# Query products of a linear-attention and two-layer kernel: four 64x64 blocks of TensorE in place of one 128x128 block-diagonal product

## The chip, the cores and the metric

The kernel runs on one core of one Trainium2 chip. The metric is the device time of one execution in microseconds (us). Before the change it is 289.2 us, the median of three runs (289.18 to 289.35).

## The reference

Inputs are q, k and v, each [8 batches, 8 heads, 576 positions, 64 channels] in float32, and the weights w_in [512, 2048] and w_out [2048, 512]. For each batch and head:

```python
q_s = softmax(q, axis=channels)
k_s = softmax(k, axis=positions)
kv  = k_s^T @ v          # 64 x 64 for each head
x   = q_s @ kv           # 576 x 64 for each head
```

The eight heads' x are laid side by side, which gives 4608 tokens of 512 channels, and then

```python
h   = x @ w_in
out = maximum(0.01 * h, h) @ w_out      # 4608 x 512, float32
```

## The kernel before

All of w_in, w_out and x (transposed: channels on partitions, tokens along the free dimension, tile `xT`) stay in on-chip memory as bf16. The two dense layers are worked through in nine tiles of 512 tokens, t = 0 to 8. In a tile, `layer1` (L459) makes sixteen blocks `ph` of 128 hidden units, each with four matmuls over the four 128-row blocks of channels; `leaky` (L469) takes each from PSUM through ScalarE into `gj`; then `layer2` (L481) makes four blocks `pout` of 128 tokens, sixteen matmuls each. The first tile is different: it covers batch 0's 576 positions, its first 256 columns are begun with half of the channel blocks (`begin`, L659) before the rest is there.

Beside this dense work the attention of the next batches is prepared. For a batch b:

- `kv` (L291; for batch 0 `kv_pair`, L368) multiplies exp(k) with v. The contraction over 64 positions of a row uses half of TensorE's rows, so two matmuls with 64 rows and 128 columns, one on each half of the rows, stand one behind the other, 36 for a batch. A product of 128x128 holds two heads on its diagonal 64x64 blocks; what is off the diagonal is not wanted.
- `kd_make` (L309; for batch 0 `kd_rec` and `kd_one`, L382 and L386) divides the diagonal blocks by the sums of exp(k) and writes them into `kd2`, four 128x128 block-diagonal tiles for a batch. The zeros off the diagonal were written once (L124). `kd_one` multiplies a whole 128x128 tile with a mask `block` (L106).
- `q_turn` (L436) turns the softmax of q so that channels lie on partitions, with a DMA transpose on SyncE's queue (for batch 0 `q_transpose` on TensorE and `q_keep`, L393 and L409).
- `attend_x` (L444; for batch 0 `attend`, L417) multiplies: one 128x128 matmul for each pair of heads and each of two parts of the positions (`XR`: 320 and 256 columns), eight for a batch, each into a PSUM tile of its own, which ScalarE (for batch 1 also VectorE) copies into `xT`.

The order is written out by hand. Each engine works through its instructions in the program's order. The `at(t, u, ...)` table hangs pieces of attention work behind unit u of tile t: units 0 to 15 are the blocks of layer 1, units 16 to 31 groups of four layer-2 matmuls. `attend_x` stands in four units, two matmuls in each, in layer 2 of some tile (L597 for batch 1: two units of four; L637 for batch 2; L619 for the others).

PSUM has two pools: `psB` with six buffers of one bank (`ph`, `pkv`, `po`, the transposes) and `psO` with two (`pout`).

At the start GpSimd's queue loads w_in with a cast from float32 to bf16, in two halves (L520, L547), each as four transfers of 64 partitions (`load_w_in`, L130). The halves are put behind parts of k by small copies into `gate`. SyncE's queue loads q, k and v of batch 0, then a small transfer `held` (L514, called at L575) that waits for the first w_in transfer of the second half, and behind it k, q and v of batch 1. GpSimd waits for batch 1's k (L579) before it issues w_out in six transfers (L141).

In this kernel channel block c of `w_in_sb` holds heads in the order that the block-diagonal tiles give (`XB`, and the rearrangement at L127), so w_in's rows are permuted when they are loaded.

Of the kernel before, what the change touches and what calls it, by code (L numbers as in the profile page):

```python
# [8 lines left out]
FP32 = mybir.dt.float32  # L9
BF16 = mybir.dt.bfloat16  # L10
AF = mybir.ActivationFunctionType
ALU = mybir.AluOpType
# [7 lines left out]
L = 64  # L20
R = 9
# [4 lines left out]
def kernel(  # L26
# [78 lines left out]
    make_identity(nc, identf)  # L105
    block = const_pool.tile([P, P], FP32)  # L106
    nc.gpsimd.memset(block, 0.0)
    for p0 in range(0, P, D):
        nc.gpsimd.memset(block[p0 : p0 + D, p0 : p0 + D], 1.0)
    warm = const_pool.tile([P, 1], BF16)  # L110
# [5 lines left out]
    xT = xT_pool.tile([P, NB, T], BF16)  # L116
    XB = (0, 2, 1, 3)


    vb2 = [const_pool.tile([P, R, 2, 130], BF16, name=f"vb{i}") for i in range(2)]  # L120
    kd2 = [const_pool.tile([P, NB, P], BF16, name=f"kd{i}") for i in range(2)]
    for i in range(2):
        nc.gpsimd.memset(vb2[i][:, :, :, 128:129], 1.0)
        nc.gpsimd.memset(kd2[i], 0.0)  # L124


    w_in_r = moe_w_in.rearrange("(gg hp hh d) f -> gg hp d hh f", gg=2, hp=2, hh=2)  # L127
    w_in_t = w_in_sb.rearrange("p (hh gg) f -> p gg hh f", gg=2)

    def load_w_in(j0, j1):  # L130
        fs = slice(j0 * P, j1 * P)
        for gg in range(2):
            for hp in range(2):
                nc.gpsimd.dma_start(  # L134
                    out=w_in_t[hp * D : (hp + 1) * D, gg, :, fs], in_=w_in_r[gg, hp, :, :, fs]
                )

# [171 lines left out]
    def kd_make(b):  # L309
        for hh in range(2):  # L310
            pkv = st[b]["pkv"][hh]
            krec = small_pool.tile([P, 2, 1], FP32, name="krec")
            nc.vector.reciprocal(out=krec, in_=pkv[:, :, 128:129])
            for hp in range(2):
                p0 = hp * D
                nc.vector.tensor_tensor(
                    out=kd2[b % 2][p0 : p0 + D, 2 * hh : 2 * hh + 2, p0 : p0 + D],
                    in0=pkv[p0 : p0 + D, :, p0 : p0 + D],
                    in1=krec[p0 : p0 + D].to_broadcast([D, 2, D]),
                    op=ALU.mult,  # L320
                )
# [63 lines left out]

    def kd_one(eng, b, gg, hh):  # L386
        pkv, krec = st[b]["pkv", gg][hh], st[b]["krec", gg, hh]
        o = kd2[b % 2][:, 2 * hh + gg]
        eng.scalar_tensor_tensor(
            out=o, in0=pkv[:, 0:P], scalar=krec, in1=block, op0=ALU.mult, op1=ALU.mult  # L390
        )

# [23 lines left out]

    def attend(b, gs, c0, n, eng, pool=psB_pool, tag=BANK_TAG):  # L417

        ps = pool.tile([P, len(gs), n], FP32, name="po", tag=tag)
        for i, g in enumerate(gs):  # L420
            nc.tensor.matmul(  # L421
                ps[:, i],
                lhsT=kd2[b % 2][:, g],
                rhs=st[b]["qT", g % 2][:, g // 2].rearrange("c r l -> c (r l)")[:, c0 : c0 + n],
                start=True,
                stop=True,
            )
        x0 = XB[gs[0]]
        o = xT[:, x0 : x0 + len(gs), b * S + c0 : b * S + c0 + n]
        if eng is nc.scalar:  # L430
            eng.copy(out=o, in_=ps)
        else:
            eng.tensor_copy(out=o, in_=ps)


    def q_turn(b, rs=ALLR):  # L436
# [6 lines left out]

    def attend_x(b, g, rs, eng):  # L444
        hh, gg = divmod(g, 2)
        n = (rs.stop - rs.start) * L
        ps = psB_pool.tile([P, n], FP32, name="po", tag=BANK_TAG)
        qX = st[b]["qX"].rearrange("c (r g) (h l) -> c g h r l", g=2, h=2)
        nc.tensor.matmul(  # L449
            ps.rearrange("p (r l) -> p r l", l=L), lhsT=kd2[b % 2][:, g], rhs=qX[:, gg, hh, rs]  # L450
        )
        c0 = b * S + rs.start * L
        o = xT[:, XB[g], c0 : c0 + n]
        if eng is nc.scalar:
            eng.copy(out=o, in_=ps)  # L455
        else:
            eng.tensor_copy(out=o, in_=ps)

    def layer1(j, ph, c0, n, part=slice(0, 4), first=True, last=True):  # L459
        for i, cb in list(enumerate((0, 2, 1, 3)))[part]:  # L460
            nc.tensor.matmul(  # L461
                ph,
                lhsT=w_in_sb[:, cb, j * P : (j + 1) * P],
                rhs=xT[:, XB[cb], c0 : c0 + n],
                start=(i == 0 and first),
                stop=(i == NB - 1 and last),
            )
# [87 lines left out]
    for hh in range(2):  # L555
        kd_rec(0, 0, hh)
        kd_one(nc.vector, 0, 0, hh)
    q_keep(nc.scalar, 0, 0, 4, (0,))
    attend(0, [0, 2], 0, 256, nc.scalar)
    wake(2)  # L560
# [4 lines left out]
    kd_rec(0, 1, 1)  # L565
    kd_one(nc.vector, 0, 1, 0)
    kd_one(nc.vector, 0, 1, 1)
    q_exp(0, R1)
# [13 lines left out]


    at(0, 9, lambda: attend(0, [0, 2], 256, 256, nc.scalar))
    at(0, 9, lambda: attend(0, [1, 3], 256, 256, nc.vector))
    at(0, 9, lambda: attend(0, [0, 2, 1, 3], 512, 64, nc.scalar, psO_pool, "pout"))
    at(0, 15, lambda: k_begin(1), lambda: q_begin(1), lambda: k_tree(1, H0), lambda: k_tree(1, H1))
# [8 lines left out]
    at(0, 43, lambda: q_turn(1, XR[1]), lambda: load_all(2))  # L596
    for i in range(8):  # L597
        eng = (nc.scalar, nc.vector)[i % 2]
        at(0, (45, 46)[i // 4], lambda i=i, eng=eng: attend_x(1, (0, 2, 1, 3)[i % 4], XR[i // 4], eng))

# [4 lines left out]
    def plan(b, o):  # L605
        t = b - 2
        at(t, o, lambda: k_begin(b), lambda: q_begin(b), lambda: k_tree(b, ALLH))
        at(t, o + 3, lambda: k_allmax(b), lambda: k_sub(nc.gpsimd, b, ALLH))
        at(t, o + 7, lambda: q_max(b, ALLR), lambda: q_sub(nc.gpsimd, b, ALLR))
        at(t, o + 11, lambda: k_exp(b, ALLH))  # L610
        at(t, o + 12, lambda: v_cast(nc.gpsimd, b, 0), lambda: v_cast(nc.gpsimd, b, 1))
        at(t, o + 16, lambda: q_exp(b, ALLR))
        at(t, o + 18, lambda: q_sum(b, ALLR))
        at(t, o + 21, lambda: q_norm(b, ALLR))
        kvu, pu = o + 25, o + (33 if b == 3 else 34)
        at(t, kvu, lambda: kv(b))
        at(t, kvu + 1, lambda: kd_make(b))
        at(t, o + 22, lambda: q_turn(b))
        for i in range(8):  # L619
            at(t, pu + i // 2, lambda i=i: attend_x(b, i // 2, XR[i % 2], nc.scalar))  # L620


    def plan2():
# [12 lines left out]
        at(1, 24, lambda: kd_make(b))  # L636
        for i in range(8):  # L637
            at(1, 28 + i // 2, lambda i=i: attend_x(b, i % 4, XR[i // 4], nc.scalar))

# [25 lines left out]
    for j in range(0, 8, 2):  # L665
        begin(j)
        if j == 2:
            attend(0, [1, 3], 0, 256, nc.scalar)
    q_exp(0, R2)
# [90 lines left out]
```

## Time and profile before

| What | Value |
|---|---|
| median of three runs | 289.2 us |
| span of the profiled execution | 287.8 us |
| outside that span (289.2 less 287.8) | 1.4 us |
| TensorE matmul (PE) busy | 277.4 us, 96%, 1620 instructions |
| VectorE (DVE) busy | 148.9 us, 52% |
| ScalarE (ACT) busy | 148.1 us, 51% |
| GpSimd (POOL) busy | 85.6 us, 30% |
| L449 matmuls `po<-qX,kd` | 56 instructions, 11.1 us busy, mean 286 ns |
| L421 matmuls `po<-qT,kd` (batch 0) | 12 instructions |
| L298 matmuls `pkv<-vb,ke` (64 rows) | 252 instructions |
| granted TensorE clock | 1.00 throughout the span |

Matmuls are pipelined: one that the profile shows with 379 ns for 512 columns starts 216 ns after the one before it. So it is starts that are to be compared, not the durations of single matmuls. A few matmul records are missing from the trace; weight loads (PEld) are complete. The chain of work that ended last follows the releasers back from the last instruction and puts every stretch of the span down to an engine and line.

### The profile page before, as it was taken

The numbers are of one execution on the slowest core, as the hardware profiler recorded it, in microseconds if no ns is written. First come the engines' busy times: TensorE is split into PE (matmuls) and PEld (weight loads), VectorE is DVE, ScalarE is ACT, GpSimd is POOL, SyncE is SP. The second block draws the span as 40 slices with busy tenths as digits, with TensorE's granted clock in tenths as the row PEclk, the third lists the DMA queues.
The fourth block names the chain that finished last, engine by engine and source line by source line (L and its number), as shares of the span: only waits on it lengthen the run. The fifth ranks groups of instructions, "written<-read, shape, count | busy, mean of one in ns | idle before, by whom it ended". The sixth has DMA issues, their size and how long they took to land.

```text
span 287.8 us, 4248 instructions
## 1 busy us (share of the span) xinstructions
PE 277.4 (96%) x1620; PEld 138.6 (48%) x1646; DVE 148.9 (52%) x246; ACT 148.1 (51%) x273; POOL 85.6 (30%) x70
## 2 busy tenths in 40 slices
PE   8689999999999999999999999999999999999995
PEld 3267645555444544454454445454455444444443
DVE  2996975987960993588085727563621100110011
ACT  4976881685269218913764358434843066016400
POOL 4734560026078019406900590049100000000000
PEclk9999999999999999999999999999999999999999
DMA  7999996999959166943496239913141310131033
GB/s 247 321 207 361 271 190 153 394 292 354 173 132 400 36 136 155 397 99 76 91 394 163 67 80 356 219 36 81 30 82 36 75 36 1 39 85 24 0 73 75
DMA packets 38932, 46.35 MB, mean 161 GB/s; under 512 B 18304, under 2 KB 21632, under 8 KB 38912
## 3 DMA queue, kind: packets, MB, share of 16 engines
q1 hardware_dynamic: 35456, 41.75, 49.6%
q0 software_dynamic: 3296, 4.20, 8.4%
q8 instruction: 13, 0.21, 0.3%
q10 hardware_dynamic: 160, 0.13, 0.1%
q14 instruction: 7, 0.06, 0.1%
HBM read 36.70 MB, written 9.44 MB: 160 GB/s over the span
## 4 chain that ended last, share of the span: by engine, by line
PE 90%; DMA 3%; issue 1%; DVE 1%; POOL 1%; ACT 0%; ACTq 0%; POOLq 0%
PE pout L482 43%; PE ph L461 41%; DMA w_in_sb<-in_moe_w_in_dram 3%; PE pkv L298 3%; PE po L449 2%; DVE k_raw L364 1%; POOL w_in_sb L134 0%; ACT gj L470 0%; PE po L421 0%; ACT xT L455 0%; DVE out_sb L476 0%; POOL gate L546 0%; ACTq L470 0%; POOLq L546 0%
## 5 line engine op out<-in xcount | busy, mean ns | idle before, releaser
L482 PE MATMUL pout<-w_out_sb,gj 128*128 128x512 bf16 (+2 forms) x580 | 129.1, 373 | 0.7 <-issue 0.2
L461 PE MATMUL ph<-xT,w_in_sb 128*128 128x512 bf16 (+3 forms) x627 | 126.6, 357 | 2.3 <-DMA w_in_sb<-in_moe_w_in_dram 1.2
L470 ACT ACTIVATE gj<-ph 128x512 bf16<-128x512 f32 (+2 forms) x152 | 83.5, 582 | 55.7 <-PE ph L461 53.9
L461 PEld LDWEIGHTS <-w_in_sb 128*128 128x128 bf16 x640 | 62.1, 98 | 63.5 <-issue 2.4
L482 PEld LDWEIGHTS <-gj 128*128 128x128 bf16 x592 | 57.1, 98 | 62.1
L476 DVE COPY out_sb<-pout 128x512 f32<-128x512 f32 (+1 forms) x34 | 22.7, 674 | 85.2 <-PE pout L482 79.0
L196 POOL TENSOR_TENSOR k_raw<-k_raw,kall 128x2304 f32<-128x2304 f32 x5 | 25.3, 5064 | 76.7 <-DVE kall L188 50.4
L455 ACT CAST xT<-po 128x320 bf16<-128x320 f32 (+1 forms) x52 | 18.2, 402 | 48.6 <-PE po L449 48.6
L276 DVE TENSOR_REDUCE qsum<-qe 128x36 f32<-128x2304 bf16 (+4 forms) x11 | 19.8, 1798 | 32.6 <-ACT qe L267 32.6
L259 POOL TENSOR_TENSOR q_raw<-q_raw,qmax 128x2304 f32<-128x2304 f32 (+3 forms) x10 | 29.7, 2973 | 20.3 <-DVE qmax L228 20.2
L283 DVE TENSOR_TENSOR qe<-qe,qrec 128x2304 bf16<-128x2304 bf16 (+4 forms) x12 | 21.9, 1826 | 0.4
L204 ACT ACTIVATE ke<-k_raw 128x2304 bf16<-128x2304 f32 (+2 forms) x11 | 17.5, 1594 | 8.6 <-POOL k_raw L196 8.5
L228 DVE TENSOR_REDUCE qmax<-q_raw 128x36 f32<-128x2304 f32 (+4 forms) x11 | 19.6, 1790 | 0.1
L267 ACT ACTIVATE qe<-q_raw 128x2304 bf16<-128x2304 f32 (+4 forms) x11 | 16.8, 1526 | 1.1 <-POOL q_raw L259 0.9
L216 POOL CAST vb<-v_raw 128x1152 bf16<-128x1152 f32 x13 | 14.6, 1147 | 0.0
L449 PE MATMUL po<-qX,kd 128*128 128x320 bf16 (+1 forms) x56 | 11.1, 286 | 0.1
L327 PE MATMUL pout<-zero 128*128 128x512 bf16 x27 | 9.1, 475 | 1.3 <-POOL zero L101 1.3
L163 DVE TENSOR_TENSOR t<-k_raw 128x1024 f32<-128x1024 f32 (+1 forms) x10 | 10.1, 1011 | 0.5 <-DMA k_raw<-in_k_dram 0.2
L163 DVE TENSOR_TENSOR t<-t 128x256 f32<-128x256 f32 (+2 forms) x20 | 9.6, 478 | 0.7
L476 ACT COPY out_sb<-pout 128x512 f32<-128x512 f32 (+1 forms) x3 | 1.6, 544 | 14.2 <-PE pout L482 14.2
L298 PEld LDWEIGHTS <-ke 64*128 64x128 bf16 x252 | 7.2, 93 | 3.0 <-ACT gj L470 1.7
L449 PEld LDWEIGHTS <-kd 128*128 128x128 bf16 x56 | 5.5, 98 | 6.2
(61 smaller groups left out, 104.6 us busy)
## 6 DMA issues: line engine op xcount, KB each, us to landing
out_dram<-out_sb SPq DMA_DIRECT2D x70, 128.0 KB, 2.4
q_raw<-in_q_dram SPq DMA_DIRECT2D x7, 1152.0 KB, 8.4
v_raw<-in_v_dram SPq DMA_DIRECT2D x7, 1152.0 KB, 11.6
k_raw<-in_k_dram SPq DMA_DIRECT2D x6, 1152.0 KB, 5.9
k_raw<-in_k_dram SPq DMA_DIRECT2D x4, 576.0 KB, 5.8
w_in_sb<-in_moe_w_in_dram POOLq DMA_DIRECT2D x8, 256.0 KB, 7.1
v_raw<-in_v_dram SPq DMA_DIRECT2D x2, 576.0 KB, 7.6
w_out_sb<-in_moe_w_out_dram POOLq DMA_DIRECT2D x4, 256.0 KB, 9.3
```

Source lines behind the costliest of these rows:

```text
L163: nc.vector.tensor_tensor(out=o, in0=i0, in1=i1, op=ALU.max)
L196: eng.tensor_tensor(out=ks, in0=ks, in1=st[b]["kall"][:, hs].unsqueeze(2).to_broadcast([P, n, R, D]), op=ALU.subtract,)
L228: nc.vector.tensor_reduce(out=m, in_=st[b]["q"][:, :, rs], axis=AX.X, op=ALU.max)
L259: eng.tensor_tensor(out=qs, in0=qs, in1=st[b]["qmax", rs.start].unsqueeze(3).to_broadcast([P, HL, n, D]), op=ALU.subtract,)
L276: nc.vector.reduce_sum(out=qsum, in_=st[b]["qe"][:, rs], axis=AX.X)
L283: nc.vector.tensor_tensor(out=qes, in0=qes, in1=st[b]["qrec", rs.start].unsqueeze(3).to_broadcast([P, n, HL, D]), op=ALU.mult,)
L449: nc.tensor.matmul(ps.rearrange("p (r l) -> p r l", l=L), lhsT=kd2[b % 2][:, g], rhs=qX[:, gg, hh, rs])
L455: eng.copy(out=o, in_=ps)
L461: nc.tensor.matmul(ph, lhsT=w_in_sb[:, cb, j * P : (j + 1) * P], rhs=xT[:, XB[cb], c0 : c0 + n], start=(i == 0 and first), stop=(i == NB - ...
L470: nc.scalar.activation(out=o, in_=ph, func=AF.Prelu, alpha=LEAKY_SLOPE)
L476: copy(out=out_sb, in_=pout)
L482: nc.tensor.matmul(pout, lhsT=g_sb[j // 2][:, j % 2, tsub * P : (tsub + 1) * P], rhs=w_out_sb[:, j, os], start=(j == 0), stop=(j == NF - 1),)
```

## The change

- `kd2` holds only the diagonal 64x64 blocks: tiles of [128, 4, 64] in place of [128, 4, 128]. The mask `block`, its memsets and the zeroing of `kd2` are gone. `kd_one` is two VectorE instructions of 64x64 in place of one of 128x128.
- Each matmul of `attend` and `attend_x` on a 128x128 block-diagonal tile becomes two on 64x64 blocks. `quads` issues four together: two halves of the rows (hp) times two halves of the columns (hh), each with its own 64x64 weights and its own moving data. The two row halves write to different PSUM tiles, the two column halves to different partitions of one tile.
- The order of heads in `xT` becomes the natural one, so w_in's rows are no longer permuted: `load_w_in` issues two transfers of 128 partitions in place of four of 64, four in all in place of eight.
- `attend_x` takes a list of parts. Batches 3 to 7 do all sixteen matmuls in one unit, with six PSUM tiles of `psB`, and the six copies (four of 320 columns, two of 2x256) behind them on ScalarE. Batch 1 and batch 2 do one part in each of two units. Batch 0's late part is two groups of 320 columns in place of pieces of 256 and 64.

```diff
-    kd2 = [const_pool.tile([P, NB, P], BF16, name=f"kd{i}") for i in range(2)]
+    kd2 = [const_pool.tile([P, NB, D], BF16, name=f"kd{i}") for i in range(2)]
...
-    w_in_r = moe_w_in.rearrange("(gg hp hh d) f -> gg hp d hh f", gg=2, hp=2, hh=2)
-    w_in_t = w_in_sb.rearrange("p (hh gg) f -> p gg hh f", gg=2)
+    w_in_r = moe_w_in.rearrange("(c p) f -> p c f", p=P)
...
-        for gg in range(2):
-            for hp in range(2):
-                nc.gpsimd.dma_start(
-                    out=w_in_t[hp * D : (hp + 1) * D, gg, :, fs], in_=w_in_r[gg, hp, :, :, fs]
-                )
+        for cs in (slice(0, 2), slice(2, 4)):
+            nc.gpsimd.dma_start(out=w_in_sb[:, cs, fs], in_=w_in_r[:, cs, fs])
...
+    def quads(b, gg, ps, src, shape=None):
+
+        for hp in range(2):
+            for hh in range(2):
+                o = ps[hp][hh * D : (hh + 1) * D]
+                nc.tensor.matmul(
+                    o if shape is None else shape(o),
+                    lhsT=kd2[b % 2][hp * D : (hp + 1) * D, 2 * hh + gg],
+                    rhs=src(hh)[hp * D : (hp + 1) * D],
+                    start=True,
+                    stop=True,
+                )
+
+    def attend(b, gg, c0, n, engs, pool=psB_pool, tag=BANK_TAG):
+
+        ps = [pool.tile([P, n], FP32, name="po", tag=tag) for _ in range(2)]
+        qT = st[b]["qT", gg]
+        quads(b, gg, ps, lambda hh: qT[:, hh].rearrange("c r l -> c (r l)")[:, c0 : c0 + n])
+        for hp in range(2):
+            move(engs[hp], xT[:, 2 * gg + hp, b * S + c0 : b * S + c0 + n], ps[hp])
...
+    def attend_x(b, parts, engs):
+
         qX = st[b]["qX"].rearrange("c (r g) (h l) -> c g h r l", g=2, h=2)
...
+        made = []
+        for i in parts:
+            rs = XR[i]
+            n = (rs.stop - rs.start) * L
+            cols = slice(b * S + rs.start * L, b * S + rs.stop * L)
+            per = 512 // n
+            for g0 in range(0, 2, per):
+                ps = [psB_pool.tile([P, per, n], FP32, name="po", tag=BANK_TAG) for _ in range(2)]
+                for gg in range(g0, g0 + per):
+                    quads(
...
+                for hp in range(2):
+                    c = 2 * g0 + hp
+                    made.append((xT[:, c : c + 2 * per - 1 : 2, cols], ps[hp]))
+        for i, (o, p) in enumerate(made):
+            move(engs[i % len(engs)], o, p)
...
-    at(0, 9, lambda: attend(0, [0, 2], 256, 256, nc.scalar))
-    at(0, 9, lambda: attend(0, [1, 3], 256, 256, nc.vector))
-    at(0, 9, lambda: attend(0, [0, 2, 1, 3], 512, 64, nc.scalar, psO_pool, "pout"))
+    at(0, 9, lambda: attend(0, 0, 256, 320, (nc.scalar, nc.vector)))
+    at(0, 9, lambda: attend(0, 1, 256, 320, (nc.scalar, nc.vector), psO_pool, "pout"))
...
-    for i in range(8):
-        eng = (nc.scalar, nc.vector)[i % 2]
-        at(0, (45, 46)[i // 4], lambda i=i, eng=eng: attend_x(1, (0, 2, 1, 3)[i % 4], XR[i // 4], eng))
+    for i in range(2):
+        at(0, (45, 46)[i], lambda i=i: attend_x(1, (i,), (nc.scalar, nc.vector)))
...
-        for i in range(8):
-            at(t, pu + i // 2, lambda i=i: attend_x(b, i // 2, XR[i % 2], nc.scalar))
+        at(t, pu + 1, lambda: attend_x(b, (0, 1), (nc.scalar,)))
...
-        for i in range(8):
-            at(1, 28 + i // 2, lambda i=i: attend_x(b, i % 4, XR[i // 4], nc.scalar))
+        for i in range(2):
+            at(1, 28 + 2 * i, lambda i=i: attend_x(b, (i,), (nc.scalar,)))
```

More of the change, by code (lines that the diff above doesn't have):

```diff
@@ L105 @@
     make_identity(nc, identf)
[L106 to L109, printed above, removed]
     warm = const_pool.tile([P, 1], BF16)
@@ L116 @@
     xT = xT_pool.tile([P, NB, T], BF16)
-    XB = (0, 2, 1, 3)
     vb2 = [const_pool.tile([P, R, 2, 130], BF16, name=f"vb{i}") for i in range(2)]
-    kd2 = [const_pool.tile([P, NB, P], BF16, name=f"kd{i}") for i in range(2)]
+    kd2 = [const_pool.tile([P, NB, D], BF16, name=f"kd{i}") for i in range(2)]
     for i in range(2):
         nc.gpsimd.memset(vb2[i][:, :, :, 128:129], 1.0)
-        nc.gpsimd.memset(kd2[i], 0.0)
-    w_in_r = moe_w_in.rearrange("(gg hp hh d) f -> gg hp d hh f", gg=2, hp=2, hh=2)
-    w_in_t = w_in_sb.rearrange("p (hh gg) f -> p gg hh f", gg=2)
+    w_in_r = moe_w_in.rearrange("(c p) f -> p c f", p=P)
     def load_w_in(j0, j1):
         fs = slice(j0 * P, j1 * P)
-        for gg in range(2):
-            for hp in range(2):
-                nc.gpsimd.dma_start(
-                    out=w_in_t[hp * D : (hp + 1) * D, gg, :, fs], in_=w_in_r[gg, hp, :, :, fs]
-                )
+        for cs in (slice(0, 2), slice(2, 4)):
+            nc.gpsimd.dma_start(out=w_in_sb[:, cs, fs], in_=w_in_r[:, cs, fs])
     w_out_r = moe_w_out.rearrange("(fb f) o -> f fb o", f=P)
@@ L316, in kd_make @@
                 nc.vector.tensor_tensor(
-                    out=kd2[b % 2][p0 : p0 + D, 2 * hh : 2 * hh + 2, p0 : p0 + D],
+                    out=kd2[b % 2][p0 : p0 + D, 2 * hh : 2 * hh + 2],
                     in0=pkv[p0 : p0 + D, :, p0 : p0 + D],
@@ L384, in kd_rec, with kd_one @@
         nc.vector.reciprocal(out=krec, in_=st[b]["pkv", gg][hh][:, 128:129])
-    def kd_one(eng, b, gg, hh):
+    def kd_one(b, gg, hh):
         pkv, krec = st[b]["pkv", gg][hh], st[b]["krec", gg, hh]
[L388 to L391, printed above, removed]
+        for hp in range(2):
+            rows = slice(hp * D, (hp + 1) * D)
+            nc.vector.tensor_scalar(
+                out=kd2[b % 2][rows, 2 * hh + gg],
+                in0=pkv[rows, hp * D : (hp + 1) * D],
+                scalar1=krec[rows],
+                scalar2=None,
+                op0=ALU.mult,
+            )
     def q_transpose(b, r0, n):
@@ L415, in q_keep, with move @@
                 eng.tensor_copy(out=o, in_=i)
[L417 to L429, printed above, removed]
+    def move(eng, o, i):
         if eng is nc.scalar:
-            eng.copy(out=o, in_=ps)
+            eng.copy(out=o, in_=i)
         else:
-            eng.tensor_copy(out=o, in_=ps)
+            eng.tensor_copy(out=o, in_=i)
+    def quads(b, gg, ps, src, shape=None):
[8 more added lines that the diff above has]
+                    stop=True,
+                )
+    def attend(b, gg, c0, n, engs, pool=psB_pool, tag=BANK_TAG):
[4 more added lines that the diff above has]
+            move(engs[hp], xT[:, 2 * gg + hp, b * S + c0 : b * S + c0 + n], ps[hp])
     def q_turn(b, rs=ALLR):
@@ L442, in q_turn @@
         )
[L444 to L447, printed above, removed]
+    def attend_x(b, parts, engs):
         qX = st[b]["qX"].rearrange("c (r g) (h l) -> c g h r l", g=2, h=2)
[L449 to L457, printed above, removed]
+        made = []
[8 more added lines that the diff above has]
+                    quads(
+                        b,
+                        gg,
+                        [p[:, gg - g0] for p in ps],
+                        lambda hh: qX[:, gg, hh, rs],
+                        lambda o: o.rearrange("p (r l) -> p r l", l=L),
+                    )
+                for hp in range(2):
+                    c = 2 * g0 + hp
+                    made.append((xT[:, c : c + 2 * per - 1 : 2, cols], ps[hp]))
+        for i, (o, p) in enumerate(made):
+            move(engs[i % len(engs)], o, p)
     def layer1(j, ph, c0, n, part=slice(0, 4), first=True, last=True):
-        for i, cb in list(enumerate((0, 2, 1, 3)))[part]:
+        for i in range(NB)[part]:
             nc.tensor.matmul(
                 ph,
-                lhsT=w_in_sb[:, cb, j * P : (j + 1) * P],
-                rhs=xT[:, XB[cb], c0 : c0 + n],
+                lhsT=w_in_sb[:, i, j * P : (j + 1) * P],
+                rhs=xT[:, i, c0 : c0 + n],
                 start=(i == 0 and first),
@@ L556 @@
         kd_rec(0, 0, hh)
-        kd_one(nc.vector, 0, 0, hh)
+        kd_one(0, 0, hh)
     q_keep(nc.scalar, 0, 0, 4, (0,))
-    attend(0, [0, 2], 0, 256, nc.scalar)
+    attend(0, 0, 0, 256, (nc.scalar, nc.scalar))
     wake(2)
@@ L565 @@
     kd_rec(0, 1, 1)
-    kd_one(nc.vector, 0, 1, 0)
-    kd_one(nc.vector, 0, 1, 1)
+    kd_one(0, 1, 0)
+    kd_one(0, 1, 1)
     q_exp(0, R1)
@@ L667 @@
         if j == 2:
-            attend(0, [1, 3], 0, 256, nc.scalar)
+            attend(0, 1, 0, 256, (nc.scalar, nc.scalar))
     q_exp(0, R2)
```

## The prediction

> **What bounds the kernel now.** I read the chain of work that ended last first, then TensorE's waits, then single stretches of the timeline. The page's chain:
>
> ```profile
> PE 90%; DMA 3%; issue 1%; DVE 1%; POOL 1%; ACT 0%; ACTq 0%; POOLq 0%
> ...
> L449 PE MATMUL po<-qX,kd 128*128 128x320 bf16 (+1 forms) x56 | 11.1, 286 | 0.1
> ```
>
> 90% of the span is TensorE. From the 25 us mark to the end TensorE hardly waits, so there each removed 0.1 us of TensorE is 0.1 us of the span. The L449 row shows 56 products with only 0.1 us of idle time before them: they stand on the path, among dense work. What one visit to them costs is in the timeline of batch 3 (start, us, what):
>
> ```profile
> 106.07 0.41 PE L449 MATMUL po<-qX,kd 128*128 128x320 bf16 x2
> 106.32 1.03 PE L482 MATMUL pout<-w_out_sb,gj 128*128 128x512 bf16 x4
> ```
>
> Two products, 320 and 256 columns, take 106.07 to 106.32, 0.245 us: by their single starts 0.136 and 0.109. They cause no gap. A batch has four such visits, 0.98 us. Next, the one kind of work here that already uses parts of the array, kv on row halves (TensorE around batch 1's kv):
>
> ```profile
> 41.60 0.81 PE L482 MATMUL pout<-w_out_sb,gj 128*128 128x512 bf16 x3
> 42.35 1.20 PE L298 MATMUL pkv<-vb,ke 64*128 64x129 bf16 x36
> 43.47 0.82 PE L482 MATMUL pout<-w_out_sb,gj 128*128 128x512 bf16 x2
> ```
>
> The third L482 starts at 42.03 (its row ends at 42.41 and one lasts 0.379) and hands over 0.216 later, at 42.25; dense work resumes at 43.47. The visit costs 1.22 us. Its pairs start 0.056 apart, so 18 pairs are 1.01: both halves do run side by side, and the other **0.21 us is the price of going into the divided array and back**, the same in all seven batches. Two column halves are seen in the start-up (kall, 128 rows by 64 columns):
>
> ```profile
> 9.22 0.44 PE L353 MATMUL kallp<-identf,kr 128*64 128x128 f32 x4 [0.38 <-DVE kr L348]
> 9.22 0.20 PEld L353 LDWEIGHTS kallp<-identf,kr 128*64 128x64 f32 x4 [0.77 <-DVE kr L348]
> ```
>
> Four products and four loads. The last product lasts 0.273, so it starts at 9.39, and the four starts lie 0.006, 0.153 and 0.007 apart: the two column halves run together too, in two rounds. A lone L338 of 128 f32 columns holds TensorE for 0.165; four in a row would need 0.66.
>
> Last, the start and one stall (TensorE from 20.3; the batch 2 to tile 2 handover, ACT and PE):
>
> ```profile
> 21.74 1.91 PE L461 MATMUL ph<-xT,w_in_sb 128*128 128x256 bf16 x16 [0.85 <-DMA w_in_sb<-in_moe_w_in_dram]
> 23.48 0.50 PE L397 MATMUL psum_qt<-ident,qe 128*128 128x128 bf16 x6
> 24.35 0.60 PE L461 MATMUL ph<-xT,w_in_sb 128*128 128x256 bf16 x4 [0.37 <-DMA w_in_sb<-in_moe_w_in_dram]
> 24.79 0.72 PE L421 MATMUL po<-qT,kd 128*128 128x256 bf16 x8
> 25.34 0.49 PE L461 MATMUL ph<-xT,w_in_sb 128*128 128x256 bf16 x3
> ```
>
> ```profile
> 79.60 0.65 ACT L455 CAST xT<-po 128x256 bf16<-128x256 f32 x2 [0.44 <-PE po L449]
> ```
>
> TensorE twice waits for w_in, so whatever precedes 21.74 has 0.85 us of cover. At 79.5 a tile's first matmul is followed by the next only at 80.02, 0.51 later instead of 0.216: 0.30 us lost to the last copy of batch 2.
>
> **The change, part by part.** The sum is made on the profiled execution: span 287.8, and 1.4 outside it to the 289.2 of the median, which I leave alone.
>
> *Products.* Sixteen quarters stand for eight products. If four run together a batch has four rounds, 2 x 0.136 + 2 x 0.109 = 0.49 us instead of 0.98. Each visit adds a price of switching. No row has 64x64; the nearest are kv, 0.21, and the step from kall back to full matmuls, 9.39 to 9.59, which is 0.05 more than a round. Bounds 0.05 and 0.42 (one kv price for each direction of division). I take 0.21 for the switch, since kv stands in the same dense surroundings, and add 0.03 for the first 64-column loads, half the 0.055 between kall's two loads on one column half.
> - Batches 3 to 7, one visit: -0.49 + 0.24 = -0.25 each, -1.25 in all.
> - Batch 1, two visits: -0.49 + 0.48 = 0.0.
> - Batch 2, two visits: 0.0. Its stall shrinks: after the second visit four layer-2 matmuls (0.86) now follow, and ACT needs two copies of 512 columns (0.58 each, as L431). The first channel block is there in time, the second some 0.13 late: -0.17.
> - Batch 0, late group (24.79): four products of 256 and four of 64, 0.55 us, become two rounds and one switch, 0.27 + 0.24 = 0.51: -0.04. Its two early groups lie ahead of 21.74.
>
> One page weighs against these rounds. The Trainium skill, "TensorE: Matmul & The Clock Gate", Part 3 ("The mechanism"), says that a weight load overlaps running matmuls only where the row group differs, and two quarters of a four share one. By kv's rows the load for a row half starts 2 ns after that same half's matmul has started, so the trace does not agree. By the rule the sum would lose the gain; that is the second rival.
>
> *Copies.* For a batch ACT had 4 x 0.43 + 4 x 0.38 = 3.24 us, now 4 x 0.43 + 2 x 0.58 = 2.88, in one burst. Behind it waits leaky of the next tile. Batches 5 to 7 have eleven units of 0.86 us until then, batch 4 six. Batch 3 has two, 1.7 us, and 0.86 for the first block: about when the burst ends; six psB buffers cover the rest, and the first four copies, all that tile 3 reads, end before it. psB is free in layer 2 (batch 1 has four buffers, and its second visit comes 0.86 later than the first two copies of 0.43 and 0.49 need). Cost 0; without the cover up to 0.5.
>
> *kd_one.* Four DVE instructions of 0.35 become eight of 64x64, between L384 (one column, 0.16) and L316 (64x128, 0.29); at 0.22 that is +0.36 on DVE. ACT gets two copies of 256 (0.39) for one of 512 (0.58), twice: +0.4. Both lie before the 0.85 us wait; uncovered they would cost 0.4. The 1.6 us of memsets on POOL precede its 4.0 us wait for k: 0.
>
> *w_in.* POOL issues two transfers for four. The w_out rows of 128 partitions take 0.74, w_in's 0.61: 1.5 us instead of 2.4, beside the first half's running packets. The same bytes move. From 12 to 21.5 the queue view shows w_in alone on the DMA engines at their limit, so the landing is set by bytes. The wait at 21.74 needs the same half of channel blocks as before. One engine that also fetched 16 KB of instructions at 19.33 lands last, 21.61 against 20.25 for the rest; I expect it there again. A 256-row transfer may start 0.35 later (first w_out packet 3.65 after issue, w_in's 3.3): +0.15. Against this, `held` waits for a whole half of the second load: released at some 21.6 instead of 19.0. So batch 1's k starts after w_in's tail and no longer shares with it; the 0.37 wait mostly goes. What is late next is the qT copies (ACT 24.50, then DVE 24.89), which hold the late group near its old place. Sum for the start: 0.0, bounds -1.0 (no late engine) and +0.9.
>
> Queued behind `held` are k, q and v of batch 1, and w_out behind k. k comes some 0.6 later, q 1.15. DVE idles 1.69 us before L276 at 42.33, which takes that up. w_out's first pieces have landed at 33.4 and 35.94 and are wanted at 35.2 and 36.9; a shift of 0.4 to 0.6 fits.
>
> Sum: -1.25 + 0.0 - 0.17 - 0.04 + 0.0 = **-1.46 us: span 286.4, time 287.7**.
>
> **The rivals.**
> 1. *Fours do not run as four.* If the two column halves of a row half take turns (they need different moving data; in kall both read identf), a batch keeps 0.98 us and pays the switches: +0.24 x 5, +0.48, +0.48 - 0.17, +0.24 for batch 0: +2.2, **291.4, slower**. It decides from a round of 0.136 becoming 0.19: 30 rounds x 0.05 take the whole 1.5 us. For it: no row shows both divisions at once. Against it: kall's starts 6 ns apart.
> 2. *Loads are not hidden*: each round waits for one load of 0.055 (30 x 0.055 = 1.65: **289.4, no change**) or two, one after the other (3.3: **291.0, slower**). Against it: the 2 ns in kv. This is what the rule of the Trainium skill cited above would do here.
> 3. *The switch is dearer*, 0.42 instead of 0.24: ten visits on the path, +1.8: 289.5, no change.
> 4. *The start decides.* No late engine: -1.0, 286.7. Or the third transfer and what follows come 0.9 later: 288.6.
>
> **How the numbers follow.** Forecast 0.58 (287.0 to 288.4); no change by 2 or 3: 0.13; slower by 1 or 2: 0.17; start better 0.06, start worse 0.06 (half of it no longer faster than the bound). A measurement here can tell about 0.2%, 0.6 us. Faster: 0.58 + 0.06 + 0.03 + 0.01 (the near end of rival 3) = 0.68; same 0.12 + 0.03 = 0.15; slower 0.17. The range takes in the better start and no change, 286.6 to 289.5; the slower cases stay outside.
>
> **What would show it.** Right: in the changed profile the sixteen quarters of batch 5 lie within 0.5 us by starts, fours some 5 ns apart, dense matmuls resume 0.7 after their due time, the total of PE starts falls by 0.25 a batch. Wrong: starts within a four 0.05 or more apart (rival 1), rounds of 0.19 to 0.25 (rival 2), a gap over 0.3 at either edge (rival 3), a w_in wait beyond 21.9 or a new wait for w_out at 35 (rival 4).

## The result, and the profile after

The changed kernel takes **288.6 us** (median of 13 runs, 288.45 to 288.83) against 289.2 for the kernel before in the same comparison (13 runs, 288.87 to 289.46). The ratio is 0.9981, 95% interval [0.9972, 0.9989]: faster by 0.6 us, where 1.5 was forecast. The profiled execution has a span of 287.0 us (before: 287.8) and took 288.8, near the upper end of these runs.

The gain and what ate it lie in different places. Taking the same weight loads in both traces, this is how much later (+) or earlier (-) the changed kernel reaches them:

| Point | after less before, us |
|---|---|
| layer 1 resumes behind batch 0's late group (25.34 before) | +0.64 |
| first matmul of layer 2 (35.21) | +0.65 |
| tile 1 begins (batch 1's products done) | +0.62 |
| tile 2, layer 2 (batch 2's done) | +0.42 |
| tile 4 begins (batches 3 and 4 done) | -0.10 |
| tile 7 begins (batch 7's done) | -0.88 |

From the end of the start to tile 7, 1.52 us are won; the start loses 0.64. In a second profiled execution of the changed kernel (after_again, below) the first row reads +0.40 and the last -1.12: 1.52 are won again, and its whole start lies 0.25 earlier.

The won part first. A *visit* is one stay of TensorE at a batch's query products, between two stretches of dense matmuls. TensorE around batch 3's single visit in the changed kernel (each row: start, us from the first start to the last end, what):

```profile
104.77 2.75 PE L495 MATMUL pout<-w_out_sb,gj 128*128 128x512 bf16 x12
107.45 0.68 PE L423 MATMUL po<-qX,kd 64*64 64x320 bf16 x16
108.07 1.90 PE L495 MATMUL pout<-w_out_sb,gj 128*128 128x512 bf16 x8
```

The last dense matmul before the visit starts at 107.144 (its row ends 0.379 later), so dense work resumes 0.926 after it, where 0.216 is due: 0.71 us for sixteen quarters (64x64 matmuls), where eight 128x128 products took 0.976. By single starts the four quarters of a round lie 3 to 4 ns apart, and the rounds start 0.160, 0.136 and 0.109 after one another. Batch 2's last two copies, which answer to the 79.60 row of before:

```profile
79.32 1.07 ACT L414 CAST xT<-po 128x512 bf16<-128x512 f32 x2 [0.90 <-PE po L423]
```

The first of the two is there in time. The second ends at 80.39, and tile 2's second matmul starts 0.352 behind its first instead of 0.216: a loss of 0.14 is left of 0.30.

Now the start. The chain that ended last no longer goes over w_in's transfers. Its two lines:

```profile
PE 91%; DVE 4%; issue 0%; ACT 0%
PE pout L495 44%; PE ph L474 42%; PE pkv L287 3%; PE po L423 2%; DVE kd L380 1%; DVE k_raw L353 1%; DVE qe L272 1%; DVE qmax L217 1%; DVE q_raw L248 0%; PE psum_qt L392 0%; DVE qT L410 0%; DVE qsum L265 0%; ACT qT L408 0%; DVE krec L373 0%; DVE out_sb L489 0%
```

DMA had 3% of it before and now has none; VectorE's share went from 1% to 4%, and among its lines stands `kd` L380, which is `kd_one`. TensorE in the same stretch (the last row is cut by the window):

```profile
18.14 0.62 PE L423 MATMUL po<-qT,kd 64*64 64x256 bf16 x3 [0.20 <-DVE kd L380]
...
22.00 0.40 PE L392 MATMUL psum_qt<-ident,qe 128*128 128x128 bf16 x4 [0.52 <-DVE qe L272]
22.23 1.91 PE L474 MATMUL ph<-xT,w_in_sb 128*128 128x256 bf16 x16
...
25.19 0.85 PE L423 MATMUL po<-qT,kd 64*64 64x320 bf16 x8
25.97 1.27 PE L474 MATMUL ph<-xT,w_in_sb 128*128 128x256 bf16 x10
```

Twice TensorE waits for VectorE. Where the row of before waited 0.85 for w_in at 21.74, the same matmuls now start at 22.23 without a wait for w_in: their turn came late, because the transposes in front of them waited for `qe` until 22.00. Before, these transposes came at 20.51:

```profile
20.51 0.39 PE L397 MATMUL psum_qt<-ident,qe 128*128 128x128 bf16 x4
```

VectorE's list shows why. Before:

```profile
14.51 0.35 DVE L389 SCALAR_TENSOR_TENSOR kd<-pkv,krec,block 128x128 bf16<-128x128 f32 x1
...
14.97 0.35 DVE L389 SCALAR_TENSOR_TENSOR kd<-pkv,krec,block 128x128 bf16<-128x128 f32 x1
...
16.35 0.61 DVE L389 SCALAR_TENSOR_TENSOR kd<-pkv,krec,block 128x128 bf16<-128x128 f32 x2
...
19.68 0.69 DVE L283 TENSOR_TENSOR qe<-qe,qrec 128x512 bf16<-128x512 bf16 x1
```

and after:

```profile
14.46 0.60 DVE L380 TENSOR_SCALAR kd<-pkv,krec 64x64 bf16<-64x64 f32 x2
...
15.29 0.60 DVE L380 TENSOR_SCALAR kd<-pkv,krec 64x64 bf16<-64x64 f32 x2
...
17.18 1.23 DVE L380 TENSOR_SCALAR kd<-pkv,krec 64x64 bf16<-64x64 f32 x4
...
21.25 0.69 DVE L272 TENSOR_TENSOR qe<-qe,qrec 128x512 bf16<-128x512 bf16 x1
```

A row of several shows the time that they share: two 128x128 take 0.61 together, 0.267 from start to start. A 64x64 one, a quarter of the elements, is followed by the next 0.308 to 0.323 later. So the old four held VectorE for 4 x 0.267 = 1.07 us, the new eight for 2.52: **+1.45 us**, and `qe`, behind them, starts 1.57 later.

On TensorE the transposes come 1.49 later (22.00 against 20.51) and the dense work behind them 0.49 (22.23 against 21.74): 1.0 us went into the place of the old wait for w_in, the cover, and the rest came through.

The wait for w_in itself was gone. The trace marks the landing of a w_in transfer sixteen times, once for each DMA engine, and TensorE goes on behind the last mark; one that lies far behind the others is called a late engine here. Before, the last engine of the sixth of eight transfers, which TensorE needed at once, landed at 21.61, the one before it at 20.25. After, the transfer with a late engine was the fourth of four (23.10, the one before it 22.52), and the third, which TensorE needs at 22.23, was complete at 19.97. In both executions an instruction fetch of 16 KB, 0.9 us long, lies ahead of this (19.33 before, 19.44 after). That the late engine is the one that fetched is inferred from these times; the trace does not name the engines. The missing wait did not add to the loss: even a third transfer at 21.2, as in wide_kd below, would have been in time for 22.23.

### The profile page after: what moved, and what is told of

Read it like the earlier page. It is cut to its first block, busy times and chain, and to the rows that moved or that the text cites. A ratio compares the mean times of both kernels' runs of the same rounds, so it can differ in the third digit from the quotient of the medians.

```text
span 287.0 us, 4376 instructions
## 1 busy us (share of the span) xinstructions
PE 278.5 (97%) x1706; PEld 134.5 (47%) x1706; DVE 150.5 (52%) x250; ACT 146.0 (51%) x262; POOL 82.3 (29%) x61
## 4 chain that ended last, share of the span: by engine, by line
PE 91%; DVE 4%; issue 0%; ACT 0%
PE pout L495 44%; PE ph L474 42%; PE pkv L287 3%; PE po L423 2%; DVE kd L380 1%; DVE k_raw L353 1%; DVE qe L272 1%; DVE qmax L217 1%; DVE q_raw L248 0%; PE psum_qt L392 0%; DVE qT L410 0%; DVE qsum L265 0%; ACT qT L408 0%; DVE krec L373 0%; DVE out_sb L489 0%
## 5 line engine op out<-in xcount | busy, mean ns | idle before, releaser
L495 PEld LDWEIGHTS <-gj 128*128 128x128 bf16 x592 | 56.3, 98 | 66.4 <-issue 1.9
L414 ACT CAST xT<-po 128x320 bf16<-128x320 f32 (+2 forms) x45 | 18.0, 486 | 47.8 <-PE po L423 47.8
L316 PE MATMUL pout<-zero 128*128 128x512 bf16 x28 | 9.0, 450 | 1.3 <-POOL zero L101 1.3
L305 DVE TENSOR_TENSOR kd<-pkv,krec 64x128 bf16<-64x128 f32 x28 | 8.1, 289 | 0.8
L287 PE MATMUL pkv<-vb,ke 64*128 64x129 bf16 x252 | 8.4, 216 | 0.0
```

The lines of the kernel that those rows point to most:

```text
L287: nc.tensor.matmul(pkv[hh][:, gg, 0:129], lhsT=st[b]["ke"][rows, r, 2 * gg : 2 * gg + 2].rearrange("p h d -> p (h d)"), rhs=vb2[b % 2][row ...
L414: eng.copy(out=o, in_=i)
L495: nc.tensor.matmul(pout, lhsT=g_sb[j // 2][:, j % 2, tsub * P : (tsub + 1) * P], rhs=w_out_sb[:, j, os], start=(j == 0), stop=(j == NF - 1),)
```

## The experiments

All times are medians; "after" is the changed kernel, and "before" in a row is the kernel before, run beside it on the same chip. Ratios are to that.

| Kernel | us | before, us | ratio [95% interval] | profiled span |
|---|---|---|---|---|
| after | 288.59 | 289.18 | 0.9981 [0.9972, 0.9989] | 287.0 |
| kd_act | 287.82 | 289.39 | 0.9950 [0.9937, 0.9964] | 286.1 |
| kd_act_w8 | 287.91 | 289.39 | 0.9948 [0.9936, 0.9961] | 286.1 |
| two_visits | 289.98 | 289.39 | 1.0022 [1.0013, 1.0032] | 288.2 |
| before_kd8 | 290.16 | 289.39 | 1.0030 [1.0018, 1.0041] | 288.7 |
| wide_kd | 288.56 | 289.33 | 0.9974 [0.9963, 0.9985] | 287.4 |
| wide_kd_b2 | 288.99 | 289.33 | 0.9987 [0.9978, 0.9995] | 287.9 |
| after_again | 288.64 | 289.33 | 0.9979 [0.9970, 0.9988] | 286.7 |
| wide_kd_w8 | 287.72 | 289.21 | 0.9947 [0.9935, 0.9960] | 285.9 |
| wide_kd_again | 288.27 | 289.21 | 0.9971 [0.9959, 0.9983] | 286.5 |
| kd_act_again | 287.34 | 289.21 | 0.9934 [0.9922, 0.9947] | 285.6 |
| kd_act_b2s | 287.39 | 289.21 | 0.9935 [0.9922, 0.9947] | 285.6 |
| kd_order | 288.29 | 289.18 | 0.9968 [0.9956, 0.9981] | 286.1 |

The profiled executions do not begin alike: the first kv product of batch 0 starts between 13.16 and 13.84 us. Counted from there, dense work behind batch 0's late group resumes, against before, 0.69 us later in after, after_again and two_visits, 0.54 later in before_kd8, 0.02 later in kd_order, and 0.53 earlier in all four executions with kd_act's edit. In the four with wide_kd's edit, where a late engine keeps the dense work waiting for w_in, it is 0.08 to 0.38 earlier.

### kd_act: half of kd_one taken off VectorE

```diff
-            nc.vector.tensor_scalar(
-                out=kd2[b % 2][rows, 2 * hh + gg],
-                in0=pkv[rows, hp * D : (hp + 1) * D],
...
+            o, i = kd2[b % 2][rows, 2 * hh + gg], pkv[rows, hp * D : (hp + 1) * D]
+            if hp == 0:
+                nc.vector.tensor_scalar(
+                    out=o, in0=i, scalar1=krec[rows], scalar2=None, op0=ALU.mult
+                )
+            else:
+                nc.scalar.activation(out=o, in_=i, func=AF.Copy, scale=krec[rows])
```

> The changed kernel, with the lower 64 rows of each kd block of batch 0 scaled on ScalarE (an activation with Copy and a per-row scale) and only the upper 64 rows on VectorE: four 64x64 VectorE instructions fewer in the start. Theory (VectorE's longer list at the start took the place of the w_in wait): VectorE's list falls by 4 x 0.30 = 1.2 us, the transposes of batch 0's rows 4 and 5 start near 20.8 instead of 22.0, dense matmuls after the late group resume near 24.8 instead of 25.97, and the time falls by 0.8 to 1.2 us against the changed kernel (288.59), to some 287.5. Rival (the start is later because of the quarters' own switches, the split copies on ScalarE or the later load of batch 1): no change within 0.2 us, 288.6.

Measured: ratio 0.9950 where after has 0.9981, and 0.9934 in a second comparison (kd_act_again), so 0.9 to 1.4 us less than after. TensorE's start of kd_act:

```profile
20.89 0.39 PE L392 MATMUL psum_qt<-ident,qe 128*128 128x128 bf16 x4
21.11 1.91 PE L474 MATMUL ph<-xT,w_in_sb 128*128 128x256 bf16 x16
...
24.71 3.52 PE L474 MATMUL ph<-xT,w_in_sb 128*128 128x256 bf16 x27
```

The transposes start 1.11 us earlier than in after and dense work resumes at 24.71 instead of 25.97; from there on the two kernels run alike but for one wait in kd_act, 0.31 us at 36.76 for w_out's second piece (it landed at 36.72). The load that VectorE carried at the start is what the change lost.

### before_kd8: only kd_one of the change, in the kernel before

```diff
-        o = kd2[b % 2][:, 2 * hh + gg]
-        eng.scalar_tensor_tensor(
-            out=o, in0=pkv[:, 0:P], scalar=krec, in1=block, op0=ALU.mult, op1=ALU.mult
-        )
+        for hp in range(2):
+            rows, cols = slice(hp * D, (hp + 1) * D), slice(hp * D, (hp + 1) * D)
+            eng.tensor_scalar(
+                out=kd2[b % 2][rows, 2 * hh + gg, cols],
+                in0=pkv[rows, cols],
+                scalar1=krec[rows],
...
```

> The kernel before, with kd_one alone split: two VectorE instructions of 64x64 that write the diagonal blocks, in place of one of 128x128 with the mask (128x128 products, eight w_in transfers, all else as before). Theory (VectorE's list): eight instructions at a pace of 0.30 put the transposes of rows 4 and 5 at 21.9 instead of 20.5 and dense work after the late group 0.4 to 0.6 later: 289.6 to 289.8. Rival (the 0.85 us wait for w_in covers it): no change within 0.2 us of 289.2.

Measured: 290.16 against 289.39, 0.8 us slower than before (0.3%), more than the 0.4 to 0.6 that was expected.

```profile
22.23 0.40 PE L402 MATMUL psum_qt<-ident,qe 128*128 128x128 bf16 x4 [0.64 <-DVE qe L283]
22.47 1.91 PE L466 MATMUL ph<-xT,w_in_sb 128*128 128x256 bf16 x16
```

With nothing else changed the transposes wait for `qe` until 22.23 (20.51 before) and the dense work comes at 22.47 (21.74). Of both differences 0.26 lies ahead of `kd_one`: kv of batch 0 already begins that much later in this execution. Here too no late engine met the w_in transfer that the dense work needs: the sixth was complete at 20.71, so VectorE alone set the start. This is the mechanism of after's start, alone.

### two_visits: the switch price

In after, batches 3 to 7 in two visits in place of one:

```diff
-        at(t, pu + 1, lambda: attend_x(b, (0, 1), (nc.scalar,)))
+        at(t, pu + 1, lambda: attend_x(b, (0,), (nc.scalar,)))
+        at(t, pu + 2, lambda: attend_x(b, (1,), (nc.scalar,)))
```

> The changed kernel, with batches 3 to 7 in two visits (the 320-column part, four layer-2 matmuls, the 256-column part) instead of one. Theory (the price is that of a visit: 0.22 us for going into the quartered array and back): each of the five batches takes 0.93 us of TensorE instead of 0.71, +1.1 us in all, 289.7. Rival (the price hangs on each four or on the first loads, not on the visit): within 0.3 us of 288.6.

Measured: ratio 1.0022 against after's 0.9981, 1.2 us more. Batch 3 in it:

```profile
107.47 0.47 PE L423 MATMUL po<-qX,kd 64*64 64x320 bf16 x8
107.86 1.04 PE L495 MATMUL pout<-w_out_sb,gj 128*128 128x512 bf16 x4
108.83 0.41 PE L423 MATMUL po<-qX,kd 64*64 64x256 bf16 x8
109.40 0.81 PE L495 MATMUL pout<-w_out_sb,gj 128*128 128x512 bf16 x3 [0.16 <-issue]
```

From the dense matmul before each visit to the one behind it (the visit's weight loads are complete in the trace; a dense record before the last row is missing), the visits cost 0.49 and 0.44, together 0.93 against 0.71 for one: **0.22 us for one more way into and out of the divided array**. All quarters run as fast as in after. With two visits for batches 3 to 7 the change is slower than the kernel before, although its query products take half the time.

### kd_act_w8: w_in's eight transfers

On kd_act:

```diff
-            nc.gpsimd.dma_start(out=w_in_sb[:, cs, fs], in_=w_in_r[:, cs, fs])
+            for ps in (slice(0, D), slice(D, P)):
+                nc.gpsimd.dma_start(out=w_in_sb[ps, cs, fs], in_=w_in_r[ps, cs, fs])
```

> As kd_act, but w_in in eight transfers of 64 partitions (two for each half of the channel blocks), in natural order. Theory (eight transfers release the held transfer after a quarter of the second load, batch 1's k then shares the DMA engines with w_in's tail): w_in's third quarter again complete near 21.6 and the last near 24.2, TensorE waits for it twice, and the time is 0.5 to 1.0 us longer than kd_act, near 288.3. Rival (the landing is set by the bytes and by the instruction fetch on one engine, not by the number of transfers): the same as kd_act within 0.2 us.

Measured: 287.91 against 287.82, no difference; that four transfers gain over eight did not show. TensorE's waits hold one line on w_in:

```profile
PE ph L475 <- DMA w_in_sb<-in_moe_w_in_dram: 0.2, 1, 0.2
```

In this execution the transfer with the late engine was the seventh (22.81, the one before it 21.82). The number of transfers does matter elsewhere, through `held`, as the next kernels show.

### wide_kd: the 128x128 tile back, the quarters kept

```diff
-    kd2 = [const_pool.tile([P, NB, D], BF16, name=f"kd{i}") for i in range(2)]
+    kd2 = [const_pool.tile([P, NB, P], BF16, name=f"kd{i}") for i in range(2)]
...
-        for hp in range(2):
-            rows = slice(hp * D, (hp + 1) * D)
-            nc.vector.tensor_scalar(
-                out=kd2[b % 2][rows, 2 * hh + gg],
...
+        nc.vector.scalar_tensor_tensor(
+            out=kd2[b % 2][:, 2 * hh + gg],
+            in0=pkv[:, 0:P], scalar=krec, in1=block, op0=ALU.mult, op1=ALU.mult
+        )
...
-                    lhsT=kd2[b % 2][hp * D : (hp + 1) * D, 2 * hh + gg],
+                    lhsT=kd2[b % 2][hp * D : (hp + 1) * D, 2 * hh + gg, hp * D : (hp + 1) * D],
```

The mask, its memsets and the zeroing of `kd2` are back too.

> The changed kernel with one part undone: the blocks keep their 128x128 tiles (zeroed once, mask kept), so kd_one is again one VectorE instruction of 128x128, four in the start instead of eight; the quarters read the diagonal blocks of these tiles. Theory (eight small VectorE instructions at the start cost what the quarters gain): the transposes of rows 4 and 5 start at about 20.5 to 20.9, dense work after the late group resumes near 24.7 instead of 25.97, and the time is 0.8 to 1.1 us below the changed kernel's, like kd_act. Rival (what helped in kd_act was something else, such as ScalarE's new place in the order): no change against the changed kernel.

Measured: 288.56, ratio 0.9974. On the same chip after has 0.9979 (after_again, 288.64). So the gain of 0.8 to 1.1 was not there, and by the time alone this spoke against VectorE as the cause.

> The changed kernel once more, beside the other two on one chip: 0.998 of the kernel before, some 0.6 us below it, and 0.8 to 1.1 us above wide_kd by the theory.

The trace says otherwise. Dense work resumes at 24.86, 0.47 earlier than before and 1.1 earlier than after, as the theory had it. Then, in wide_kd:

```profile
21.25 1.92 PE L474 MATMUL ph<-xT,w_in_sb 128*128 128x256 bf16 x16 [0.47 <-DMA w_in_sb<-in_moe_w_in_dram]
...
36.41 7.07 PE L495 MATMUL pout<-w_out_sb,gj 128*128 128x512 bf16 x31 [1.37 <-DMA w_out_sb<-in_moe_w_out_dram]
```

The second row is a new wait, for w_out. In this kernel the late engine, behind a 16 KB fetch at 19.17, is in the third w_in transfer: last engine 21.21, the one before it 19.92. `held` waits for that transfer and goes out at 21.22 (19.89 in kd_act), batch 1's first k lands at 25.99 (24.74), w_out is issued at 26.69 (25.31), and its first piece lands at 36.36 (33.75), when TensorE has wanted it since 35. The last 1.2 us of that are a second late engine, in w_out's first piece itself (36.36, the one before it 35.13), behind the next 16 KB fetch at 34.33. To test `held`'s part, the same kernel with eight w_in transfers (the edit of kd_act_w8), where `held` hangs on the fifth:

> wide_kd with w_in in eight transfers, as before had it. In wide_kd the start was 0.47 us earlier than before's, as taking kd_one's cost away should make it, but the first product with w_out came 1.5 us later than due: the third of the four w_in transfers landed at 21.21 (its last engine 1.3 us behind the others), `held` waits for that transfer, and batch 1's loads and w_out come behind `held` (first w_out landing 36.36, PE waits 1.37). Theory: with eight transfers `held` waits for the fifth, which lands at about 19 to 19.9, so the w_out wait of 1.4 us goes and the time falls to 287.3 to 287.9 us (0.7 to 1.3 below wide_kd). Rival: the loss lies in the 128-column tile itself (its quarters' strided loads, the memsets): then the time stays at 288.3 to 288.8.

and wide_kd once more beside it:

> wide_kd once more, to stand beside wide_kd_w8 on one chip. Theory: the late w_in engine and the w_out wait come again in most executions, 288.4 to 288.8. Rival, that the wait was an accident of one profile: 287.5 to 288.0.

Measured: 287.72 and 288.27, ratios 0.9947 and 0.9971. wide_kd_w8 lies in its range; wide_kd_again lies 0.13 below the range of its theory and 0.27 above the rival's. The first row of layer 2 in wide_kd_again, then in wide_kd_w8:

```profile
35.48 7.07 PE L495 MATMUL pout<-w_out_sb,gj 128*128 128x512 bf16 x32 [0.55 <-DMA w_out_sb<-in_moe_w_out_dram]
```

```profile
34.97 7.07 PE L496 MATMUL pout<-w_out_sb,gj 128*128 128x512 bf16 x32
```

In wide_kd_again `held` went out at 21.11 again and the wait is there again, 0.55; with eight transfers `held` goes out at 18.51, w_out's first piece lands at 33.26, and there is no wait. So kd_one costs about what kd_act showed, and wide_kd lost it again at `held`. No cost of the 128-column tile shows: wide_kd_w8 is 0.4 above kd_act_again on the same chip, but it also waits 0.78 for w_in, which kd_act_again does not.

### kd_order: why small instructions are dear

In after, the same eight kd_one instructions, the two on the upper 64 partitions first:

```diff
-    def kd_one(b, gg, hh):
+    def kd_one(b, gg, hh, hps=(0, 1)):
...
-        for hp in range(2):
+        for hp in hps:
...
     for hh in range(2):
         kd_rec(0, 0, hh)
-        kd_one(0, 0, hh)
+    for hp in range(2):
+        for hh in range(2):
+            kd_one(0, 0, hh, (hp,))
...
-    kd_one(0, 1, 0)
-    kd_one(0, 1, 1)
+    for hp in range(2):
+        for hh in range(2):
+            kd_one(0, 1, hh, (hp,))
```

> after, with the eight kd_one instructions in another order alone: the two on the upper 64 partitions first, then the two on the lower (after alternates halves). In after one on the upper half holds VectorE for 0.308 us and one on the lower for 0.322; in kd_act, where only upper ones are left, two in a row are 0.20 apart. Theory (what costs is the change of half): a group of four takes 0.20 + 0.31 + 0.20 + 0.32, about 1.03 in place of 1.26 us, so batch 0's second query part is normalised some 0.45 earlier and the time falls by 0.3 to 0.45, to 288.1 to 288.3. Rival (what costs is the lower half): the third and fourth stay at 0.31 to 0.32 each and the gain is about 0.2. Second rival (what costs is the pair on one PSUM tile): all but the last at 0.20, gain 0.6 to 0.7.

VectorE in it (three rows; the third is batch 0's second query part, at 21.25 in after):

```profile
14.29 1.00 DVE L380 TENSOR_SCALAR kd<-pkv,krec 64x64 bf16<-64x64 f32 x4
...
16.56 1.00 DVE L380 TENSOR_SCALAR kd<-pkv,krec 64x64 bf16<-64x64 f32 x4
...
20.40 0.69 DVE L272 TENSOR_TENSOR qe<-qe,qrec 128x512 bf16<-128x512 bf16 x1
```

Starts within a group lie 0.201, 0.300 and 0.208 apart, and the next instruction, on all partitions from 0, comes 0.318 after the last: a group holds VectorE for 1.03 us in place of 1.26, as the first theory had it to the hundredth. An instruction that begins on the same partition as the one before it follows after 0.20; one that begins on another waits until that one has ended (0.268 or 0.276 long, the next start at 0.300 or 0.308). The Trainium skill states this in "VectorE: DVE Perf Modes", section "Two Vector instructions with no wait between them": an instruction whose input or output starts in another group of 32 partitions than the last one's is held until every earlier VectorE instruction has finished. The trace agrees, 0.30 to 0.32 held and 0.20 to 0.21 not.

The time is 288.29, 0.3 below after (ratio 0.9968 against 0.9981), within what was expected; but the two intervals overlap, and what decides between the theories are the spacings, not the time. The profiled execution, with 287.92 near the lower end of this kernel's runs (287.86 to 288.73), shows more: `qe` 0.85 earlier than in after, of which 0.46 are the changes of half, 0.21 the two reciprocals that now follow each other, and 0.17 an earlier begin of the whole list. Why the runs spread over 0.9 us is open.

### Batch 2 in one visit: two tries

wide_kd_b2 (on wide_kd), then kd_act_b2s (on kd_act):

```diff
-        for i in range(2):
-            at(1, 28 + 2 * i, lambda i=i: attend_x(b, (i,), (nc.scalar,)))
+        at(1, 29, lambda: attend_x(b, (0, 1), (nc.scalar, nc.vector)))
```

```diff
-        for i in range(2):
-            at(1, 28 + 2 * i, lambda i=i: attend_x(b, (i,), (nc.scalar,)))
+        at(1, 28, lambda: attend_x(b, (0, 1), (nc.scalar,)))
```

> As wide_kd, and batch 2's sixteen quarters in one visit, one unit later than the first of the two, with the six copies shared between ScalarE and VectorE. Theory (a visit costs 0.22 us): 0.2 us below wide_kd, provided that the copies end before tile 2's first block wants them (two units and 0.7 us later); a stall there of up to 0.5 us is the rival, and would show as a second layer-1 matmul that starts late in tile 2.

Measured: 288.99, 0.4 more than wide_kd on the same chip. Tile 2 waits for the copies that now stand in VectorE's list behind work on batch 3's k:

```profile
81.20 13.76 PE L474 MATMUL ph<-xT,w_in_sb 128*128 128x512 bf16 x61 [0.69 <-DVE xT L416]
```

So the second try left the copies to ScalarE and went a unit earlier; kd_act stood beside it:

> kd_act with batch 2's two visits made into one at unit 28, copies on ScalarE alone (in wide_kd_b2 the one visit stood at unit 29 with copies shared by VectorE, and PE waited 0.69 us for the last copy). Theory: one visit less, 0.2 us below kd_act, and no wait, since the copies (2.5 us) end before tile 2's first product. Rival: the second half of batch 2's queries is not turned yet at unit 28, and PE waits: 0 to 1 us above kd_act.

> kd_act once more, to stand beside kd_act_b2s on one chip: 287.7 to 288.0.

Measured: 287.39 and 287.34, no difference (kd_act_again lies 0.4 below the 287.7 expected; the kernel before is 0.2 lower on this chip too, and kd_act's 0.31 wait for w_out's second piece is not there). In kd_act_b2s:

```profile
75.28 0.47 PE L423 MATMUL po<-qX,kd 64*64 64x320 bf16 x8
75.92 0.41 PE L423 MATMUL po<-qX,kd 64*64 64x256 bf16 x8 [0.17 <-DMA qX<-qe]
76.26 2.76 PE L495 MATMUL pout<-w_out_sb,gj 128*128 128x512 bf16 x12
```

No wait for copies, but the second half waits inside the visit for its transposed queries: 0.17 of idle engine, and 0.34 by starts (the third round 0.480 behind the second instead of 0.136). One visit saves 0.22, and the 0.14 stall at the copies is gone; this wait eats both. Each theory was half right. The best kernel of the study remains kd_act, at 0.9934 and 0.9950 of before, with kd_act_b2s, kd_act_w8 and wide_kd_w8 within these.

## Why the prediction was right or wrong, point by point

- **Quarters in fours**: right. Starts 3 to 4 ns apart, and after the first round (0.160) the rounds take the 0.136 and 0.109 of the whole-array products. Rival 1 (the column halves take turns) is out.
- **Loads**: right. The four loads of the second round start at 107.480 to 107.490, while the first round, on the same two row groups, runs from 107.453, and the second round starts at 107.613. Rival 2 is out, and with it, for this case, the sentence of the Trainium skill that it drew on ("TensorE: Matmul & The Clock Gate", Part 3, "The mechanism"). The same page of the Trainium skill, Part 2, "Step-by-step: what each phase is for", also lets a load go ahead if it goes to the background weight buffer; the trace fits that, but it does not show which buffer a load goes to.
- **Switch, 0.24 a visit**: right. 0.71 for one visit (forecast 0.73), 0.93 for two (0.97), 0.22 between them in two_visits. Rival 3 is out.
- **Batches 3 to 7, 1, 2**: right. -0.26 each (-0.25), -0.03 (0.0), -0.19 with the stall (-0.17). Together -1.52, where -1.42 was forecast.
- **Copies, 0**: right. No wait for them shows but the 0.14 foreseen in batch 2 (0.13).
- **kd_one: this step failed.** "At 0.22 that is +0.36 on DVE" was +1.45. The forecast took the middle between a one-column instruction and L316's duration, and for the four old instructions their duration of 0.35 where their starts lie 0.267 apart. Of the 1.09 that were missing, 0.76 are the new instructions and 0.33 the old. The step also leaned on the wait for w_in ("both lie before the 0.85 us wait") and put "0.4" on its loss: the wait did cover 1.0 by starts, but not 1.5. before_kd8 measured 0.8 for this step alone, and kd_act won 0.9 to 1.4 by taking half of the instructions away. The row that counted was in the trace of before: L316 works on 64 partitions, upper and lower in turn, and its two starts in the row below lie 0.297 apart. Eight of these less four of 0.267 would have given +1.3.

```profile
45.21 0.59 DVE L316 TENSOR_TENSOR kd<-pkv,krec 64x128 bf16<-64x128 f32 x2
```

- **w_in: wrong in its detail.** "I expect it there again" (the late engine): in after it fell on the fourth transfer, not on the third, so TensorE's wait vanished and `held` went out at 19.99, not 21.6. With kd_one at its forecast price this would probably have been rival 4's better start; kd_act, which comes nearest to that, resumes 0.62 earlier than before. As it was, VectorE held TensorE until 22.0, and the earlier w_in gave its start nothing. In wide_kd the engine was where the prediction had it, `held` went out at 21.2, near the 21.6 that it said, and "a shift of 0.4 to 0.6 fits" was then too small: batch 1's first k came 0.7 later than before, but w_out's first piece, which has a late engine of its own in both, 3.0 later in one execution and 2.0 in the other, and 1.4 and 0.5 us were waited.
- **Batch 0's late group, -0.04**: wrong, a smaller term. 25.19 to 25.97 is 0.78 us, where 24.79 to 25.34 was 0.55. Its second four waits until 25.58 for a copy on VectorE (25.17) that waits for one on ScalarE; before, smaller pieces began with what was there. So +0.23, and not by kd_one: kd_act and wide_kd also take 0.78 for this group. Against it stands the 0.37 wait for w_in ahead of it, which went as forecast.
- **Sum**: start with batch 0's late group +0.64 (-0.04 forecast), of which 0.40 stand ahead of the late group and 0.23 in it; the rest -1.52 (-1.42).

Open: what decides which w_in transfer has the late engine, and whether the instruction fetch is its cause. The fetch starts between 19.0 and 20.5 in all these kernels. The late engine is in the third of four transfers in wide_kd, wide_kd_again and wide_kd_b2, in the fourth in all others with four (by 0.35 to 1.03), and with eight in the sixth (before, wide_kd_w8) or the seventh (kd_act_w8); in before_kd8 no last engine is more than 0.25 behind the one before it. The start of the fetch alone does not decide it: 19.00 in kd_order (the fourth), 19.01 in wide_kd_b2 (the third). A kernel that moved the fetch alone was not tried.

## What to carry to other kernels

A cost that lies "under" another engine's wait has two numbers, its size and the cover's, and each needs its own row: here the size was four times the guess, and the cover took up 1.0 of 1.5 us. To price an instruction, take the spacing of starts in a row whose neighbours are alike (same partitions, same alternation), not a duration or a mean of shapes. And where divided and whole-array work alternate on TensorE, count visits before counting products.

## What the runs showed of the hardware that was not expected

- VectorE: 64x64 from PSUM follows another on the same 64 partitions after 0.20 us, on the other 64 after 0.30 to 0.32 (kd_order, after); 128x128 follows 128x128 after 0.267. Splitting each of the four into two halves that alternate more than doubled the cost here (2.52 against 1.07 us).
- Four 64x64 matmuls with different weights and, between column halves, different moving data start 3 to 4 ns apart and take the time of one (0.136 us for 320 columns, as one 128x128 product); going into the divided array and back costs 0.22 us.
- Behind a 16 KB instruction fetch (0.9 to 1.0 us) one of the sixteen DMA engines of a w_in transfer often landed late, in wide_kd 1.3 us after the one before it (21.21 against 19.92). Through a transfer that others hang on, and a second such engine in w_out, that became a wait of 1.4 us on TensorE. That the fetch delays the engine is inferred from the times; in before_kd8 a fetch at 19.79 left no such mark.
